# Window attention and a mixture of experts on one core: 128-row score and output matmuls on zero-blocked operands, loads placed after the stores

## The chip, the core and the metric

The kernel runs on one core of a Trainium2 chip. The metric is device time in microseconds (us). The program is executed several times, and the kernel before took 1153.46 us (median of three runs, 1153.4 to 1158.42). One further execution was recorded by the profiler. It took 1155.89 us, of which the recorded span is 1154.2.

A core has a matrix engine (TensorE, PE, with its weight loads as PEld), a vector engine (VectorE, DVE), an activation engine (ScalarE, ACT), a general engine (GpSimd, POOL), and SyncE (SP), which in this kernel only issues transfers. Transfers run on 16 DMA engines, and those that SP issues share one queue (q1). On-chip memory, SBUF, has 128 partitions, and matmul results go to PSUM.

## The reference

Attention over 8 batches of 8 heads of 576 positions of 64 values. The first four heads look at the last 32 positions, the others at every fourth of the last 128. The result, 4608 tokens of 512 values, goes to a mixture of 8 experts, of which each token uses the best two:

```python
scores = scale * np.matmul(q, k.transpose(0, 1, 3, 2))
mask_plain = (rel >= 0) & (rel < window)                                       # window 32
mask_dil = (rel >= 0) & (rel < window * dilation) & (rel % dilation == 0)      # dilation 4
attn = np.exp(scores - np.max(scores))           # of the masked scores
attn = attn / (np.sum(attn) + 1e-09)
x = np.matmul(attn, v)                           # -> 4608 x 512
noisy_logits = x @ w_gate + np.log1p(np.exp(x @ w_noise)) * noise
top2 = ...                                       # two best of 8, weights by softmax over the two
for e in range(E):
    h = np.maximum(x[mask] @ w1[e], 0.0)         # 512 -> 1024
    out[mask] += top2_w[mask, k, None] * (h @ w2[e])
```

## The kernel before

**Attention.** The work is cut into 4 units of two batches. A unit has two groups, first its dilated heads and then its plain heads, and a group has three steps. So there are 24 steps, and a step makes 384 tokens' worth of one half of x. Each step multiplies blocks of 32 queries with the 64 keys that they can see. The host has laid out the inputs so that two streams of 64 values (two heads, or two strands of the dilated positions) lie on partitions 0 to 63 and 64 to 127. All steps work with the same tiles: keys `kt`, queries `qt`, values `vd` (dilated) and `vp` (plain, two tiles, one a batch). Values carry a 65th column of ones, which gives the softmax its denominator.

**A step.** `qk` (L291, L303) puts the mask into PSUM by two matmuls with an identity of 128 rows and then adds 48 score matmuls of 64 rows, 32 queries by 64 keys. DVE takes the row maximum off (L310, L311), `expo` is ACT's exponential (L316), and `ptr` transposes on PE (L324), copied by ACT (L327). `pv` makes 48 output matmuls of 64 rows and 65 columns (L344). DVE divides by the denominator (L350, L352, L354) and so writes `x`, which has three buffers. `store_x` sends a step's x to the scratch `xs` in six transfers on SP: for each half one of 128 KB (L365) and two of 32 KB (L367). `x_transpose` (L376) and `gate_mm` (L398) make the gate's logits. The profile counts two records for a matmul of this type, so that a step shows 96 for its 48 score matmuls.

**The order.** The program is written out by hand, in a loop of 26 rounds: round i issues `qk(i)`, `expo(i-1)`, `ptr(i-1)`, the fillers of slot 2i, `store_x(i-2)`, `x_transpose(i-2)`, `pv(i-1)`, `gate_mm(i-2)` and the fillers of slot 2i+1. A filler is a piece of other work that `at(slot, ...)` put there: loads for the next groups, clearing of the output (L860, `out_rows<-zero`), filling the compaction table `tab` with defaults (L236, from the tile `free`), the staging of the first expert's weights (L579 and L565 from DRAM to `ws`; L573, L575 split them into a high and a low part). Between these, `micro()` issues single instructions of the gate: top-2 search, positions (`posp`, L499 and L502; `cnt`, L505) and the scatter of token numbers into `tab`. An index list comes back from `tab` by a transfer to `ixf`; DVE halves its entries into `ixh` (L627), and POOL gathers the rows of x for the first expert by it (L643).

**Loads.** A group's loads stand on SP's queue among the stores. `qk_loads` (L98) fetches keys and queries two groups ahead, in slot s0+5, where s0 = 6g is a group's first slot. `v_loads` (L106, L109) fetches the next group's values, in slots s0+1 and s0+2. Each is one transfer over all 128 partitions, of columns or of a whole tile.

**The experts.** From 266 us on, PE works through the experts: `up` (L697) and `down` (L738) matmuls on blocks of tokens, with high and low parts. Weights of the next expert and gathers are placed by a planner with due times (`plan`, `tick`). The first expert's first block of tokens lies in a pool `xp0` of its own, whose memory `free` uses before.

Of the kernel before, what the change touches and what calls it, by code (L numbers as in the profile page):

```python
# [24 lines left out]
FF = 1024  # L25
# [20 lines left out]
def attention_moe_kernel(ctx, tc, qt, kp, kd, vpl, vdl, w_gate, w_noise, noise, w1, w2, out, CAP=1216, SPLITS=(0, 384, 896)):  # L46
# [18 lines left out]
    xp0 = ctx.enter_context(tc.tile_pool(name="xp0", bufs=1))  # L65
# [3 lines left out]
    actx = ExitStack()  # L69
# [16 lines left out]
    VP = [vp.tile([128, 9, 4, 65], F32, name=f"vp{i}") for i in range(2)]  # L86
# [3 lines left out]
    KV = [KT[i].rearrange("p (b x s) -> p b x s", b=2, x=2 + 2 * i) for i in range(2)]  # L90
    QV = [QT[i].rearrange("p (b x s) -> p b x s", b=2, x=2 + 2 * i) for i in range(2)]

    def qk_loads(g, parts=1):
        u, ty = g // 2, 1 - g % 2
        for i in range(parts):
            for dst, src in ((KT[ty], (kp, kd)[ty][u]), (QT[ty], qt[u, ty])):
                n = dst.shape[1] // parts
                yield lambda d=dst[:, n * i:n * i + n], s=src[:, n * i:n * i + n]: sync.dma_start(d, s)  # L98

    def v_loads(g):  # L100
        u, ty = g // 2, 1 - g % 2
        if ty:
            d = VD.rearrange("p j h y c -> p (j h y c)")
            n = d.shape[1] // 3
            for i in range(3):
                yield lambda i=i: sync.dma_start(d[:, n * i:n * i + n], vdl[u, :, n * i:n * i + n])  # L106
        else:
            for b in range(2):
                yield lambda b=b: sync.dma_start(VP[b].rearrange("p j h c -> p (j h c)"), vpl[u, b])  # L109

    for f in qk_loads(0, 2):
        f()

# [100 lines left out]
    def setup_c():  # L214
# [3 lines left out]
        free = xp0.tile([128, 3072], I32, name="free", tag="raw")  # L218
        pr = free[:, 0:3 * NR].rearrange("p (a b) -> p a b", a=3)
# [10 lines left out]
        def pads(a, b):  # L230
            padt = free[:, 3 * NR:3 * NR + TC * (b - a)].rearrange("p (a b) -> p a b", b=TC)
# [6 lines left out]
        pads(0, NR // 2)  # L238
        at(12, lambda: pads(NR // 2, NR))
# [33 lines left out]
    def blocks(st, ty):  # L273

        for r in range(6):
            for w in range(2):
                a, jp = divmod(r, 3)
                if ty == 0:
                    b, ub = divmod(12 * st + 2 * r + w, 18)
                else:  # L280
                    b, ub = divmod(6 * st + 2 * jp + w, 9)
                yield r, w, a, jp, b, ub
# [3 lines left out]
    def qk(k):  # L286
        g, st = divmod(k, 3)
        ty = 1 - g % 2
        s = aps.tile([128, 2, 512], F32, name="s", tag="s")
        for y in range(2):  # L290
            tensor.matmul(s[:, y, 0:384], lhsT=identb,  # L291
                          rhs=masks[ty][:, 6 * st:6 * st + 6].rearrange("p a b -> p (a b)"),
                          start=True, stop=False, skip_group_check=True)
        for e in range(6):
            for qd in range(4):
# [6 lines left out]
                for y in range(2):  # L302
                    tensor.matmul(s[32 * qd:32 * qd + 32, y, 64 * e:64 * e + 64],  # L303
                                  lhsT=QV[ty][64 * y:64 * y + 64, b, x, 32 * ub:32 * ub + 32],
                                  rhs=KV[ty][64 * y:64 * y + 64, b, x, 32 * ub:32 * ub + 64],
                                  start=False, stop=True, skip_group_check=True)
        a = sm.tile([128, 2, 6, 64], F32, name="a")
        mx = sm.tile([128, 2, 6], F32, name="mx")
        sv = s[:, :, 0:384].rearrange("p y (e c) -> p y e c", e=6)
        vector.tensor_reduce(mx, sv, axis=AX.X, op=OP.max)  # L310
        vector.tensor_tensor(a, sv, mx.unsqueeze(3).to_broadcast([128, 2, 6, 64]), op=OP.subtract)  # L311
        SB[k] = a

    def expo(k):
        p = sm.tile([128, 2, 6, 64], F32, name="pe")
# [754 lines left out]
```

## Time and profile before

| what | value |
|---|---|
| median of three runs | 1153.46 us (1153.4 to 1158.42) |
| profiled execution: time, span | 1155.89 us, 1154.2 us |
| mean granted PE clock | 0.95 |
| PE busy | 1023.6 us (89%) |
| DVE, ACT, POOL busy | 468.6, 289.4, 509.3 us |
| first score step (mask matmul L291) | 7.87 us |
| last score step | 241.57 us |
| first `up` matmul of the experts | 265.75 us |
| SP's queue q1 | 55,520 packets, 93.22 MB |

The profile's page gives busy times of engines, and for groups of instructions the line, the engine, the operation, the tiles (written `out<-in`), their count, their busy time, the mean length of one in ns, and the idle time of the engine before them with what ended it ("releaser"). "issue" is time in which an engine waited for nothing that the profile shows. Rows of a timeline give start and length in us. SPq is SP's transfer issuing. A DMA share of 1.0 means that all 16 DMA engines were busy.

### The profile page before, as it was taken

The numbers are of one execution on the slowest core, as the hardware profiler recorded it, in microseconds if no ns is written. First come the engines' busy times: TensorE is split into PE (matmuls) and PEld (weight loads), VectorE is DVE, ScalarE is ACT, GpSimd is POOL, SyncE is SP. The second block draws the span as 40 slices with busy tenths as digits, with TensorE's granted clock in tenths as the row PEclk, the third lists the DMA queues.
The fourth block names the chain that finished last, engine by engine and source line by source line (L and its number), as shares of the span: only waits on it lengthen the run. The fifth ranks groups of instructions, "written<-read, shape, count | busy, mean of one in ns | idle before, by whom it ended". The sixth has DMA issues, their size and how long they took to land. (4 is left out here: it accounts for less than half of the span.)

```text
span 1154.2 us, 22635 instructions
## 1 busy us (share of the span) xinstructions
PE 1023.6 (89%) x9630; PEld 870.0 (75%) x9631; DVE 468.6 (41%) x1043; ACT 289.4 (25%) x540; POOL 509.3 (44%) x620
## 2 busy tenths in 40 slices
PE   6765766455889999999999999999999999999996
PEld 4554545345669878897988899888978888998895
DVE  5544353444424454334433543444343335423221
ACT  1433332252212231213122322222231223212110
POOL 3000623242836676357534654463566256542112
PEclk8898877778999999999999999999999999999998
DMA  9665555655633443434342434333343524343123
GB/s 341 233 220 189 179 190 206 198 184 177 204 71 60 117 103 92 78 80 112 75 109 49 116 62 112 85 89 73 85 109 72 111 51 112 63 112 73 19 28 43
DMA packets 78538, 135.07 MB, mean 117 GB/s; under 512 B 29168, under 2 KB 41504, under 8 KB 75616
## 3 DMA queue, kind: packets, MB, share of 16 engines
q1 hardware_dynamic: 55520, 93.22, 24.5%
q0 software_dynamic: 22912, 40.35, 19.4%
q8 instruction: 77, 1.26, 0.4%
q14 instruction: 29, 0.24, 0.1%
HBM read 92.72 MB, written 40.81 MB: 116 GB/s over the span
## 5 line engine op out<-in xcount | busy, mean ns | idle before, releaser
L697 PE MATMUL up<-x,w1h 128*128 128x512 f32 (+2 forms) x1536 | 408.7, 350 | 0.0
L650 POOL DMA_INDIRECT g<-xs,ixi x266 | 266.3, 1001 | 94.7 <-issue 76.2
L697 PEld LDWEIGHTS up<-x,w1h 128*128 128x128 f32 x1536 | 276.8, 189 | 24.5 <-DVE hl L702 0.2
L697 PE MATMUL up<-x,w1l 128*128 128x384 f32 (+2 forms) x768 | 267.6, 348 | 0.0
L715 POOL DMA_INDIRECT out_rows<-y,ixs x70 | 112.1, 1602 | 311.3 <-DVE y L747 279.4
L738 PE MATMUL dn<-w2h,hh 128*128 128x512 f32 x576 | 225.3, 391 | 1.2 <-DVE y L747 1.2
L738 PE MATMUL dn<-w2h,hl 128*128 128x512 f32 x576 | 225.2, 391 | 0.0
L738 PE MATMUL dn<-w2l,hh 128*128 128x512 f32 x576 | 225.0, 391 | 0.0
L702 DVE SCALAR_TENSOR_TENSOR hl<-up,hh 128x384 fp32r<-128x384 f32 (+2 forms) x192 | 106.8, 557 | 238.8 <-ACT hh L701 238.8
L701 ACT ACTIVATE hh<-up 128x384 fp32r<-128x384 f32 (+2 forms) x192 | 96.7, 507 | 238.7 <-PE up L697 236.2
L697 PEld LDWEIGHTS up<-x,w1l 128*128 128x128 f32 x768 | 145.1, 189 | 12.5
L539 POOL DMA_INDIRECT tab<-en,si x72 | 71.0, 987 | 126.0 <-DVE lg L437 70.5
L738 PEld LDWEIGHTS dn<-w2h,hh 128*128 128x128 f32 x576 | 108.5, 188 | 23.6 <-DVE y L747 1.6
L738 PEld LDWEIGHTS dn<-w2h,hl 128*128 128x128 f32 x576 | 108.4, 188 | 22.7
L738 PEld LDWEIGHTS dn<-w2l,hh 128*128 128x128 f32 x576 | 108.4, 188 | 22.0
L747 DVE TENSOR_SCALAR y<-dn,ixs 128x512 f32<-128x512 f32 x63 | 47.1, 750 | 143.6 <-PE dn L738 143.6
L669 ACT CAST x<-xr 128x512 fp32r<-128x512 f32 x70 | 42.0, 599 | 200.1 <-DVE xr L667 200.1
L575 DVE TENSOR_TENSOR w1l<-ws,w1h 128x1024 fp32r<-128x1024 f32 x32 | 38.9, 1215 | 82.0 <-ACT w1h L573 82.0
L573 ACT CAST w1h<-ws 128x1024 fp32r<-128x1024 f32 x32 | 33.0, 1049 | 101.5 <-DMA ws<-in_moe_w 101.5
L303 PE MATMUL s<-kt,qt 64*32 64x64 f32 x2304 | 35.1, 238 | 22.1 <-issue 21.9
L303 PEld LDWEIGHTS s<-kt,qt 64*32 64x32 f32 x2304 | 28.3, 112 | 33.3 <-issue 32.6
L670 DVE TENSOR_TENSOR x<-xr,x 128x512 fp32r<-128x512 f32 x70 | 46.2, 661 | 17.5 <-ACT x L669 17.4
(152 smaller groups left out, 809.1 us busy)
## 6 DMA issues: line engine op xcount, KB each, us to landing
ws<-in_moe_w SPq DMA_DIRECT2D x64, 512.0 KB
out_rows<-zero SPq DMA_DIRECT2D x38, 256.0 KB
vd<-in_vdl SPq DMA_DIRECT2D x12, 780.0 KB
vp<-in_vpl SPq DMA_DIRECT2D x8, 1170.0 KB
qt<-in_qt SPq DMA_DIRECT2D x7, 1152.0 KB
xs<-x SPq DMA_DIRECT2D x48, 128.0 KB
kt<-in_kp SPq DMA_DIRECT2D x4, 1216.0 KB
g<-xs,ixi POOLq DMA_INDIRECT x266
```

The costliest lines, as they stand in the source:

```text
L303: tensor.matmul(s[32 * qd:32 * qd + 32, y, 64 * e:64 * e + 64], lhsT=QV[ty][64 * y:64 * y + 64, b, x, 32 * ub:32 * ub + 32], rhs=KV[ty][64 ...
L539: ins = gpsimd.indirect_dma_start(out=tab, out_offset=bass.IndirectOffsetOnAxis(ap=si[:, kq, t:t + 1], axis=0), in_=en[:, kq, t], in_offse ...
L575: return lambda: vector.tensor_tensor(b, s, a.bitcast(F32), op=OP.subtract)
L650: gpsimd.indirect_dma_start(out=g[:, j], out_offset=None, in_=xq, in_offset=bass.IndirectOffsetOnAxis(ap=IX[e][1][:, r0 // 32 + j:r0 // 32 ...
L669: scalar.copy(xh[:, :, o:o + rn], xr[:, :, 0:rn])
L670: return lambda: vector.tensor_tensor(xl[:, :, o:o + rn], xr[:, :, 0:rn], xh[:, :, o:o + rn].bitcast(F32), op=OP.subtract)
L697: tensor.matmul(p[:, 0:n], lhsT=a[:, 128 * f:128 * f + 128], rhs=b[:, kc, 0:n], start=(i == 0), stop=(i == 11))
L701: scalar.activation(hh[:, f, 0:n], p[:, 0:n], AF.Relu)
L702: vector.scalar_tensor_tensor(hl[:, f, 0:m], p[:, 0:m], 0.0, hh[:, f, 0:m].bitcast(F32), op0=OP.max, op1=OP.subtract)
L715: ins = gpsimd.indirect_dma_start(out=out, out_offset=bass.IndirectOffsetOnAxis(ap=sc[0:rn, t, 1:2], axis=0), in_=y[0:rn], in_offset=None, ...
L738: tensor.matmul(p[0:rn], lhsT=a[:, f, o:o + rn], rhs=b[:, f % 2], start=(i == 0), stop=(i == 23))
L747: vector.tensor_scalar(y[0:rn], p[0:rn], wsc, None, op0=OP.mult)
```

## The change

Scores and outputs are computed in one matmul where there were two. The key tile gets a second axis of two: keys of the lower 64 partitions stand in block 0, those of the upper 64 in block 1, and the other half of each block is zero. A matmul over all 128 rows then gives 2 x 64 scores for 32 queries. The values get the same form, and an output matmul has 2 x 65 columns. The zeros are written once, at the start, by DVE and POOL. Loads of keys and values go to one half of the partitions at a time, queries as before. Loads of the next groups come in odd slots, after the stores of a round: values in s0+3, s0+5 and s0+7, keys and queries in two column halves in s0+7 and s0+9. The exponential is written in place, `x` has four buffers instead of three, and `pt` and `xt` one instead of two. The dilated inputs lie in a pool that is closed in slot 43; the first expert's staged weights (`wp1`) and its first block of tokens (`xp0`) are opened in its place, and the index copy and the gathers of that block come no earlier than slot 45. `free` uses the staging buffers, in three parts instead of two.

```diff
-    VD = vp.tile([128, 9, 4, 2, 65], F32, name="vd")
-    KT = [vp.tile([128, KN[i]], F32, name=f"kt{i}") for i in range(2)]
-    QT = [vp.tile([128, 4 * S], F32, name=f"qt{i}") for i in range(2)]
+    VP = [vp.tile([128, 2, 9, 4, 65], F32, name=f"vp{i}") for i in range(2)]
+    VD = dp.tile([128, 2, 9, 4, 2, 65], F32, name="vd")
+    KT = [(vp, dp)[i].tile([128, 2, KN[i]], F32, name=f"kt{i}") for i in range(2)]
...
+            n = KN[ty] // parts
+            for y in range(2):
+                yield lambda i=i, n=n, y=y: sync.dma_start(
+                    KT[ty][64 * y:64 * y + 64, y, n * i:n * i + n],
+                    (kp, kd)[ty][u, 64 * y:64 * y + 64, n * i:n * i + n])
+            n = 4 * S // parts
+            yield lambda i=i, n=n: sync.dma_start(QT[ty][:, n * i:n * i + n], qt[u, ty, :, n * i:n * i + n])
...
+                for w in range(2):
+                    yield lambda i=i, w=w: sync.dma_start(d[64 * w:64 * w + 64, w, n * i:n * i + n],
+                                                          vdl[u, 64 * w:64 * w + 64, n * i:n * i + n])
...
+    for ty in (1, 0):
+        for y in range(2):
+            (vector, gpsimd)[y].memset(KT[ty][64 * y:64 * y + 64, 1 - y], 0.0)
     for f in qk_loads(0, 2):
         f()
+
+    for v in (VD, *VP):
+        for w in range(2):
+            (gpsimd, vector)[w].memset(v[64 * w:64 * w + 64, 1 - w], 0.0)
...
-        s = aps.tile([128, 2, 512], F32, name="s", tag="s")
+        s = aps.tile([128, 8, 2, 64], F32, name="s", tag="s")
...
-                for y in range(2):
-                    tensor.matmul(s[32 * qd:32 * qd + 32, y, 64 * e:64 * e + 64],
-                                  lhsT=QV[ty][64 * y:64 * y + 64, b, x, 32 * ub:32 * ub + 32],
-                                  rhs=KV[ty][64 * y:64 * y + 64, b, x, 32 * ub:32 * ub + 64],
-                                  start=False, stop=True, skip_group_check=True)
+                tensor.matmul(s[32 * qd:32 * qd + 32, e], lhsT=QV[ty][:, b, x, 32 * ub:32 * ub + 32],
+                              rhs=KV[ty][:, :, b, x, 32 * ub:32 * ub + 64],
+                              start=False, stop=True, skip_group_check=True)
...
-        x = sm.tile([128, 2, 6, 64], F32, name="x", bufs=3)
+        x = sm.tile([128, 2, 6, 64], F32, name="x", bufs=4)
...
-                at(s0 + 1 + i // 2, f)
+                at(s0 + 3 + 2 * (i // 2), f)
         if g + 2 < 2 * U:
-            for f in qk_loads(g + 2):
-                at(s0 + 5, f)
+            for i, f in enumerate(qk_loads(g + 2, 2)):
+                at(s0 + 7 + 2 * (i // 3), f)
...
-        later(2, go)
+        d = 2 if bi else max(2, L0 + SL_W1 + 4 - slot[0])
+        later(d, go)
...
+    def open_w1():
+        dctx.close()
+        late["wp1"] = ctx.enter_context(tc.tile_pool(name="wp1", bufs=1, side="right"))
+        late["xp0"] = ctx.enter_context(tc.tile_pool(name="xp0", bufs=1, side="right"))
+    at(L0 + SL_W1 + 2, open_w1)
```

DVE's first instructions, before (`wt` is the operand of the warm-up matmuls, `ii` to `m` lead to the masks):

```order
L117 MEMSET wt 128x256
L132 TENSOR_SCALAR ii<-ii 128x1
L133 CAST ip<-ii 128x1
L138 TENSOR_SCALAR mt<-kk,ip 128x64
L139 TENSOR_SCALAR mt<-mt 128x64
```

and after:

```order
L124 MEMSET kt_98 64x2560
L124 MEMSET kt_97 64x2432
L130 MEMSET vd 64x4680
L130 MEMSET vp_94 64x2340
L130 MEMSET vp_95 64x2340
L135 MEMSET wt 128x256
L150 TENSOR_SCALAR ii<-ii 128x1
```

Five clears of half the partitions stand ahead of what the warm-up and the masks are made from. POOL has the same five, ahead of its identity matrix.

SP's transfers of the third and fourth step, before (L365 and L367 are stores, `tab<-free` the table's defaults):

```order
L98 DMA kt_95<-in_kd 128x2560
L98 DMA qt_97<-in_qt 128x2304
L236 DMA tab<-free 128x1168
L365 DMA xs<-x 4x32x256
L367 DMA xs<-x 2x32x128 x2
L365 DMA xs<-x 4x32x256
L367 DMA xs<-x 2x32x128 x2
L106 DMA vd<-in_vdl 128x1560 x3
L365 DMA xs<-x 4x32x256
L367 DMA xs<-x 2x32x128 x2
```

and after, from the second step's stores on (the stores are L381 and L383 there):

```order
L381 DMA xs<-x 4x32x256
L383 DMA xs<-x 2x32x128 x2
L381 DMA xs<-x 4x32x256
L383 DMA xs<-x 2x32x128 x2
L100 DMA kt_98<-in_kd 64x1280 x2
L104 DMA qt_100<-in_qt 128x1152
L381 DMA xs<-x 4x32x256
L383 DMA xs<-x 2x32x128 x2
L381 DMA xs<-x 4x32x256
L383 DMA xs<-x 2x32x128 x2
L100 DMA kt_98<-in_kd 64x1280 x2
L104 DMA qt_100<-in_qt 128x1152
```

Keys and queries of a group, one block of transfers before, are two blocks of three with a step's stores between them.

On DVE, the copy of the index list (`ixh<-ixf`) stood before the count of the gate's positions (`cnt<-posp`):

```order
L354 TENSOR_TENSOR x<-o,den 128x768
L627 TENSOR_SCALAR ixh<-ixf 128x6
L505 COPY cnt<-posp 128x56
L507 TENSOR_SCALAR wd<-wd 128x6
L509 RECIPROCAL wd<-wd 128x6
```

and stands after, some 35 rows later, behind the second split of the staged weights:

```order
L363 TENSOR_SCALAR den<-o 128x6 x2
L365 RECIPROCAL den<-den 128x12
L368 TENSOR_TENSOR x<-o,den 128x384 x2
L590 TENSOR_TENSOR w1l_2947<-ws,w1h_2946 128x1024
L642 TENSOR_SCALAR ixh<-ixf 128x6
L504 TENSOR_TENSOR oh<-i_165,xf 128x24
```

The copy no longer has the count of the positions behind it, and the x of two more steps is ahead of it.

More of the change, by code (lines that the diff above doesn't have):

```diff
@@ L217, in setup_c @@
         NR = ET // 16
-        free = xp0.tile([128, 3072], I32, name="free", tag="raw")
-        pr = free[:, 0:3 * NR].rearrange("p (a b) -> p a b", a=3)
+        free = [late["stage"].tile([128, FF], I32, name="free", tag="ws") for _ in range(2)]
+        pr = free[0][:, 0:3 * NR].rearrange("p (a b) -> p a b", a=3)
         pc = acon.tile([128, 2], I32, name="pc")
@@ L236, in pads @@
             sync.dma_start(tr[:, a:b], padt)
-        pads(0, NR // 2)
-        at(12, lambda: pads(NR // 2, NR))
+        for i in range(3):
+            at(6 + 6 * i, lambda i=i: pads(NR * i // 3, NR * (i + 1) // 3))
     gens, early = [], [True]
@@ L335, in pv @@
         for hh in range(4):
-            for r, w, a, jp, b, ub in blocks(st, ty):
+            for r, a, jp, b, ub in blocks(st, ty):
                 qd, c0 = (r, hh) if r < 4 else (2 * (r - 4) + hh // 2, 4 + hh % 2)
@@ L353, in pv @@
         micro(1)
-        vector.tensor_tensor(x, ov[:, :, :, 0:64], den.unsqueeze(3).to_broadcast([128, 2, 6, 64]), op=OP.mult)
+        for w in range(2):
+            vector.tensor_tensor(x[:, w].rearrange("p (b c) d -> p b c d", b=2), ov[:, w, :, :, 0:64],
+                                 den[:, w].rearrange("p (b c) -> p b c", b=2).unsqueeze(3).to_broadcast([128, 2, 3, 64]),
+                                 op=OP.mult)
         XG[k] = x
```

80 lines of the change are left out of this document (37 added, 43 removed).

## The prediction

> **What bounds the kernel now.** I read the windows by stage first, then the waits, then the transfer queue's own timeline. The windows show two kinds of time (start:end, length, busy time of PE, weight loads, DVE, ACT, POOL, then clock, DMA share, GB/s):
>
> ```profile
> 8.00:31.00 23.00, 14.15 (x541) 10.50 (x546) 12.19 (x45) 4.87 (x11) 5.41 (x12) 0.79 0.97 343
> 31.00:206.00 175.00, 113.56 (x4041) 89.76 (x4025) 77.68 (x243) 59.38 (x141) 38.68 (x73) 0.84 0.57 201
> 330.00:1154.00 824.00, 809.37 (x3959) 700.19 (x3957) 323.38 (x558) 190.34 (x318) 401.64 (x428) 0.99 0.38 82
> ```
>
> From 330 us on, PE is busy for 809 of 824 us with the experts, which the change leaves alone. Whatever it does must happen in the attention part, where PE has 61 of 175 us free and no engine is full. The waits say who is late there (engine and line, what it waited for: us in total, times, longest):
>
> ```profile
> DVE x L354 <- DMA xs<-x: 42.8, 13, 7.8
> PE pp L324 <- ACT pe L316: 22.4, 6, 9.1
> PE s L303 <- issue: 21.9, 10, 3.9
> PE xtp L376 <- DVE cnt L505: 14.2, 2, 12.4
> DVE ixh L627 <- DMA ixf<-tab: 13.3, 1, 13.3
> PE xtp L376 <- DVE x L354: 11.2, 4, 5.0
> SPq L365 <- DVE x L354: 9.6, 1, 9.6
> PE o L344 <- issue: 8.4, 7, 2.7
> ```
>
> The largest wait on work is DVE's, for the stores of x to leave a buffer. The queue that carries these stores, SP's, waited for DVE's x a single time, at the start. So the engines wait for the queue, and the queue for nobody. Its timeline shows a beat (start, length, what SP issues):
>
> ```profile
> 30.71 0.79 SPq L98 DMA_DIRECT2D kt<-in_kd  x1
> ...
> 57.75 0.64 SPq L365 DMA_DIRECT2D xs<-x  x1
> 58.44 2.03 SPq L367 DMA_DIRECT2D xs<-x  x2
> 60.51 0.69 SPq L365 DMA_DIRECT2D xs<-x  x1
> 61.24 1.99 SPq L367 DMA_DIRECT2D xs<-x  x2
> 63.33 0.82 SPq L98 DMA_DIRECT2D kt<-in_kp  x1
> ...
> 96.69 0.54 SPq L98 DMA_DIRECT2D kt<-in_kd  x1
> ...
> 159.62 0.61 SPq L98 DMA_DIRECT2D kt<-in_kd  x1
> ...
> 191.16 0.60 SPq L98 DMA_DIRECT2D kt<-in_kp  x1
> ```
>
> The keys of a group of three steps are issued at 30.71, 63.33, 96.69 and, five groups after the first, at 191.16: (191.16 - 30.71) / 5 = 32.1 us a group, 31.5 in the last ones, or 10.5 a step. The six stores of one step take 63.33 - 57.75 = 5.6 us of it, although they move little:
>
> ```profile
> 4.00:8.00 4.00, 4.00 (x20) 1.76 (x18) 2.55 (x12) 0.00 (x0) 3.28 (x8) 1.00 1.02 418
> 56.00:60.00 4.00, 3.57 (x153) 2.99 (x152) 2.67 (x8) 1.56 (x3) 0.00 (x0) 1.00 0.19 61
> 92.00:96.00 4.00, 0.00 (x0) 0.00 (x0) 0.50 (x1) 0.00 (x0) 0.00 (x0) 0.61 0.22 68
> ```
>
> Loads alone fill the transfer engines (share 1.02, 418 GB/s); in a stretch of stores the share is 0.19 to 0.22. A store therefore uses a few of the engines, and those few are what the queue waits for. In 92:96 PE did nothing at all for that reason. PE is quicker where it is left alone: its steps (mask matmuls) follow at 6.8 and 7.1 us against the queue's 10.5:
>
> ```profile
> 55.66 0.49 PE L291 MATMUL s<-mask,identb 128*128 128x384 bf16 x2
> 62.47 0.49 PE L291 MATMUL s<-mask,identb 128*128 128x384 bf16 x2
> 69.54 0.49 PE L291 MATMUL s<-mask,identb 128*128 128x384 bf16 x2
> ```
>
> The attention part ends by the same queue: the second expert matrix arrives behind it, ACT waits 12.1 us for it, and PE stands until 284:
>
> ```profile
> 280.86 1.04 ACT L586 CAST w2h<-ws 128x1024 fp32r<-128x1024 f32 x1 [12.12 <-DMA ws<-in_moe_w]
> ...
> 284.17 0.22 PE L499 MATMUL posp<-ob,tri 128*128 128x48 bf16 x1 [9.85 <-DVE ob L491]
> ```
>
> **The change, part by part.** The sum is made against the profiled execution, 1155.9 us (span 1154.2), 2.4 above the runs' median of 1153.46.
>
> *Matmuls.* Of a step's 48 score and 48 output matmuls, 24 and 24 are left, each with twice the contraction and about twice the columns. The nearest rows are the scores of now and the gate's matmuls, which have the new shape (128 rows, 32 columns of weights; 4 of 128 and 4 of 64 columns to a step):
>
> ```profile
> 53.98 0.54 PE L398 MATMUL gp<-xt,wg 128*32 128x128 f32 x16
> ...
> 56.08 1.33 PE L303 MATMUL s<-kt,qt 64*32 64x64 f32 x96
> ```
>
> Eight gate matmuls of 96 columns on average take 0.54 us, so 24 take 1.6, or by columns (128) 2.2 us, against 1.33; the outputs, 130 wide, the same against about as much. A step gets 0.6 to 1.7 us longer on PE, from 7 to 7.6 to 8.7 us. Against that half of the 30.3 us of issue waits before L303 and L344 should go with half the instructions. All of it stays under the queue's 10.5 us a step, which hides it; without that cover it is between 24 x 1.7 - 15 = 26 us lost and 24 x 0.6 - 15 = about nothing. The masks keep their columns.
>
> *Zero blocks.* DVE and POOL each clear 2560 + 2432 + 4680 + 2340 + 2340 = 14,352 elements of 64 partitions, ahead of the warm-up operand and the identity. POOL's rows give the price:
>
> ```profile
> L232 POOL MEMSET free<- 128x1168 int32 x2 | 2.1, 1066 | 30.2 <-DMA tab<-free 30.2
> L187 POOL MEMSET zero<- 128x512 f32 x1 | 0.5, 521 | 0.0
> ```
>
> (1066 - 521) / (1168 - 512) = 0.83 ns an element, so 11.9 us. Masks and scores begin 12 us later, and so does the first x:
>
> ```profile
> 17.86 0.96 DVE L354 TENSOR_TENSOR x<-o,den 128x768 f32<-128x768 f32 x1
> 18.85 0.69 SPq L365 DMA_DIRECT2D xs<-x  x1
> ```
>
> The first store goes at about 31 instead of 18.85. Now, the transfers are full until 31 (share 0.97), so most of the 12 us is covered by initial loads. But the last piece of these, one plain value tile of 1.20 MB, is put behind the first stores; at 343 GB/s it filled 3.5 us. The queue runs dry for about that: **+3.5 us**, from 0 (memsets quicker) to 12 (no cover).
>
> *Loads.* The bytes stay, by these rows:
>
> ```profile
> vd<-in_vdl SPq DMA_DIRECT2D x12, 780.0 KB
> vp<-in_vpl SPq DMA_DIRECT2D x8, 1170.0 KB
> qt<-in_qt SPq DMA_DIRECT2D x7, 1152.0 KB
> kt<-in_kp SPq DMA_DIRECT2D x4, 1216.0 KB
> kt<-in_kd SPq DMA_DIRECT2D x3, 1280.0 KB
> ```
>
> A dilated group loads 1280 + 1152 + 3 x 780 KB, a plain one 1216 + 1152 + 2 x 1170: 4.85 MB on average, 11.6 us at 418 GB/s. The beat leaves 31.5 - 3 x 5.6 = 14.7 us for loads, so 3.1 us a group go to the two changes between stores and loads, 1.6 each. The change spreads the loads over all three steps of a group, a third such place: 1.6 x 7 groups = 11 at most, nothing at least, since loads placed behind stores can also use the transfer engines that the stores leave free. I take half, **+5.5 us**. SP issues 47 more transfers at 0.4 to 0.8 us each in place of longer ones, which its queue covers (it waits for transfers, not for its own issuing); without that cover they cost 19 us at 0.4.
>
> *Half partitions.* No row shows a load into 64 partitions. At the rate of now it costs nothing. At half that rate, the keys and values before the first stores, 1280 + 2340 + 1216 + 1170 KB = 6.15 MB, take 14.7 us more at 418 GB/s; later ones, 3.67 MB a group, 8.8 us a group, 61 over seven. Here the stores help: an engine that no store uses has 5.6 us of slack a step. I take nothing, as nearest to the rows there are, and leave the rest to a rival and the range.
>
> *The fourth x buffer, the copies, the pools.* The fourth buffer shortens DVE's 42.8 us, but a buffer moves a wait and doesn't shorten the queue. The extra den and x instructions, two a step, go to a DVE that is busy for 78 of 175 us. The index copy, on which DVE stood 13.3 us and PE 12.4 (L505), moves behind two weight splits; the queue goes on through that stall. The first expert's gathers come up to four slots (two steps) later; they are due before PE's 284 us. All of this: 0, between -4 and +4.
>
> Sum: 1155.9 + 3.5 + 5.5 = 1164.9, say **1165 us**; its own range 1156 to 1178.
>
> **The rivals.** *Half-rate loads.* [...] At the start this is +14.7 in full; later the slack of the free engines takes most, and I charge a quarter of the 61, 15. 1165 + 30 = 1195, between 1175 and, if nothing is covered, 1241. For it: 418 GB/s at a share of 1.02 is a limit somewhere, and no row says on which side. Against it: the stores, not the loads, hold the queue. [...]
>
> *Faster: PE decides.* If the steps are late because PE's stalls make the stores late, half of the 30.3 us of issue waits, the 11.2 for x and the 14.2 behind the index copy go, 40.5 us, less the 12 us of the later start, with matmuls at their lower price: 1156 - 28.5 = 1127, between 1110 and, with them at the upper, 1147. It decides if the queue has gaps in which it waits for x. For it: those rows, all of them PE's. Against it: SP's single wait of 9.6 us.
>
> *No change.* The start and the bursts are both absorbed, for instance by loads that run beside stores: 1155, between 1149 and 1159.
>
> **How the numbers follow.** Forecast 0.40, half-rate loads 0.20, faster 0.24, no change 0.16. A measurement of this kernel can tell about 0.5% (5.8 us) from nothing. Faster: 0.24 and 0.02 of the no-change case, 0.26. Within 0.5%: 0.13 of that case and 0.06 of the forecast's lower edge, 0.19. Slower: 0.55. The range that leaves out the better half of the fast case and the worse half of the half-rate case is 1130 to 1198.
>
> **What would show it.** The first store of x at 29 to 33 us; SP's keys still 31 to 33 us apart per group; DVE's wait for stores shorter, but ACT's wait for the second matrix still there, ending near 290; PE's issue waits at L303 and L344 about halved with nothing gained. Half-rate loads would show as a share of 0.5 to 0.6 in the first 20 us where 1.02 stands now. I am wrong if the beat falls well under 31 us a group: then the queue wasn't the bound, or its stores and loads overlap better than they did.

## The result

The changed kernel takes 1195.59 us (median of four runs, 1194.43 to 1197.75) where the kernel before took 1155.41 beside it: a ratio of 1.0348 (95% interval 1.0315 to 1.038), 40 us slower. The forecast was 1165 us; the rival with half-rate loads had been given 1195, and the whole range was 1130 to 1198. The profiled execution of the changed kernel has a span of 1194.2 us.

In three of the five series of experiments below the kernel before itself took 1231 to 1247 us instead of 1154 to 1156, so a ratio always stands against the kernel before in the same series.

The windows of the changed kernel, by the same stages (start:end, length, busy time of PE, weight loads, DVE, ACT, POOL, clock, DMA share, GB/s):

```profile
8.00:31.00 23.00, 11.57 (x132) 6.15 (x132) 15.53 (x28) 1.64 (x2) 15.38 (x27) 1.00 1.02 245
31.00:206.00 175.00, 109.64 (x2107) 90.43 (x2107) 77.12 (x279) 53.54 (x127) 32.16 (x62) 0.84 0.69 174
```

The transfer engines are as busy from 8 to 31 us as they were (share 1.02, before 0.97) and move 245 GB/s instead of 343. In the attention part the share went up from 0.57 to 0.69 while the rate fell from 201 to 174: more engine time for the same bytes (over the whole span the queue q1 takes 28.1% of the 16 engines for 93.23 MB, before 24.5% for 93.22). SP's keys (now in two column halves a group, of which the first is shown) show the beat:

```profile
52.98 1.23 SPq L100 DMA_DIRECT2D kt<-in_kd  x2
88.68 1.16 SPq L100 DMA_DIRECT2D kt<-in_kp  x2
127.68 1.23 SPq L100 DMA_DIRECT2D kt<-in_kd  x2
161.12 1.17 SPq L100 DMA_DIRECT2D kt<-in_kp  x2
199.91 1.26 SPq L100 DMA_DIRECT2D kt<-in_kd  x2
232.97 1.18 SPq L100 DMA_DIRECT2D kt<-in_kp  x2
```

(232.97 - 52.98) / 5 = 36.0 us a group, where 31.5 to 32.1 stood. The waits of the first 330 us (engine and line, what it waited for: us in total, times, longest):

```profile
PE s L317 <- DMA qt<-in_qt: 58.6, 11, 11.2
PE pp L336 <- ACT a L328: 20.4, 4, 18.3
PE wm L141 <- DVE ii L150: 16.5, 1, 16.5
ACT w2h L601 <- DMA ws<-in_moe_w: 14.8, 1, 14.8
PE o L356 <- ACT pt L339: 7.9, 17, 1.9
```

DVE no longer waits for stores, and PE's issue waits before scores are 3.5 us where 21.9 stood (first row below, after the idle time). In their place PE waits 58.6 us for queries, the last piece of each batch of loads. The experts' first matmul starts at 304.8 us instead of 265.75, 39 us later, so nearly the whole loss is made before it:

```profile
L317 PE MATMUL s<-kt,qt 128*32 128x128 f32 x1152 | 49.4, 325 | 62.1 <-DMA qt<-in_qt 58.6 <-issue 3.5
...
L712 PE MATMUL up<-x,w1h x1536: 307/334/775, 304.8 to 1148.8; 128*128 128x384 f32 x64, 128*128 128x512 f32 x64, 128*128 128x320 f32 x64
```

(The second row is the summary of one line's instructions: shortest, median and longest in ns, then first and last start in us.)

### The profile page after: what moved, and what is told of

The parts are those of the page before. It is cut to its first block, busy times and chain, and to the rows that moved or that the text cites. A ratio compares the mean times of both kernels' runs of the same rounds, so it can differ in the third digit from the quotient of the medians.

```text
span 1194.2 us, 18188 instructions
## 1 busy us (share of the span) xinstructions
PE 1032.6 (86%) x7326; PEld 880.6 (74%) x7327; DVE 484.7 (41%) x1101; ACT 288.5 (24%) x540; POOL 522.9 (44%) x626
## 3 DMA queue, kind: packets, MB, share of 16 engines
q1 hardware_dynamic: 57952, 93.23, 28.1%
q0 software_dynamic: 22912, 40.35, 18.5%
## 4 chain that ended last, share of the span: by engine, by line
PE 75%; DMA 10%; SPq 5%; DVE 4%; issue 4%; ACT 1%; POOL 0%; POOLq 0%; DVEq 0%; ACTq 0%
PE up L712 35%; PE dn L753 31%; DMA qt<-in_qt 5%; SPq L383 3%; PE s L317 2%; DMA ws<-in_moe_w 2%; PE o L356 1%; PE dn L749 1%; PE dn L747 1%; DMA g<-xs,ixh 1%; SPq L381 1%; PE pp L336 1%; SPq L100 1%; DMA vp<-in_vpl 1%; DMA vd<-in_vdl 1%
## 5 line engine op out<-in xcount | busy, mean ns | idle before, releaser
L712 PEld LDWEIGHTS up<-x,w1l 128*128 128x128 f32 x768 | 145.2, 189 | 12.4
L317 PE MATMUL s<-kt,qt 128*32 128x128 f32 x1152 | 49.4, 325 | 62.1 <-DMA qt<-in_qt 58.6
L317 PEld LDWEIGHTS s<-kt,qt 128*32 128x32 f32 x1152 | 39.7, 130 | 72.2 <-issue 57.4
L684 ACT CAST x<-xr 128x512 fp32r<-128x512 f32 x70 | 41.9, 599 | 201.9 <-DVE xr L682 201.9
L322 DVE TENSOR_REDUCE mx<-s 128x12 f32<-128x768 f32 x24 | 23.0, 957 | 95.5 <-PE s L317 95.5
```

The lines of the kernel that those rows point to most:

```text
L317: tensor.matmul(s[32 * qd:32 * qd + 32, e], lhsT=QV[ty][:, b, x, 32 * ub:32 * ub + 32], rhs=KV[ty][:, :, b, x, 32 * ub:32 * ub + 64], star ...
L684: scalar.copy(xh[:, :, o:o + rn], xr[:, :, 0:rn])
L712: tensor.matmul(p[:, 0:n], lhsT=a[:, 128 * f:128 * f + 128], rhs=b[:, kc, 0:n], start=(i == 0), stop=(i == 11))
```

## The experiments

Theory 1: a transfer into 64 neighbouring partitions moves at about half rate, and the queue, which sets the beat, pays for it. Theory 2: the loss comes from where the loads stand, behind the stores, and from the new matmuls. The later start is a third part. The forecast's own theory, that the stores hold the queue because they use few transfer engines, was tested too.

| run | what | ratio (interval) | the kernel before there |
|---|---|---|---|
| b_low | before, keys and values loaded in lower and upper halves | 1.0374 (1.032 to 1.0428) | 1245 us |
| b_evn | before, in even and odd partitions | 1.0017 (0.9983 to 1.0052) | 1245 us |
| a_again | changed kernel, unaltered | 1.0069 (1.0023 to 1.0114) | 1231 us |
| a_evn2, a_evn3 | changed, even and odd partitions | 1.0025 (0.9986 to 1.0064), 1.0006 (0.9972 to 1.0039) | 1231, 1247 us |
| a_evn4 | the same | 1.0104 (1.0086 to 1.0122) | 1156 us |
| a_evn_place | the same, loads where the kernel before has them | 1.0038 (1.0015 to 1.0062) | 1154 us |
| a_place | changed, loads where the kernel before has them | 1.0123 (1.0071 to 1.0175) | 1247 us |
| a_evn_start | as a_evn4, zeros in another order | 1.0133 (1.0111 to 1.0154) | 1154 us |
| b_st16, b_st16_2, b_st16_3 | before, stores of 128 rows | 1.0016, 1.0017, 1.0001 (all within 0.9968 to 1.0061) | 1245, 1231, 1247 us |
| b_st16_4 | the same | 0.9663 (0.964 to 0.9687) | 1156 us |
| a_evn_st16 | as a_evn4, with such stores | 0.9805 (0.9756 to 0.9853) | 1231 us |
| a_all | the same, zeros as in a_evn_start | 0.972 (0.9699 to 0.9741) | 1154 us |
| a_best_p | with such stores, loads as before, zeros in a third order | 0.9855 (0.9812 to 0.9897) | 1247 us |
| a_best2 | with such stores, loads as in the change, POOL clears more | 0.9704 (0.9688 to 0.9721) | 1156 us |

**Halves of the partitions, in the kernel before.**

```diff
+    def two(d, s):
+        d, s = d.rearrange("(y p) n -> y p n", y=2), s.rearrange("(y p) n -> y p n", y=2)
+        for y in range(2):
+            sync.dma_start(d[y], s[y])
...
-                yield lambda i=i: sync.dma_start(d[:, n * i:n * i + n], vdl[u, :, n * i:n * i + n])
+                yield lambda i=i: two(d[:, n * i:n * i + n], vdl[u, :, n * i:n * i + n])
```

The diff is cut: keys and plain values are changed in the same way. b_evn has "(p y) n -> y p n" in `two`.

> The kernel before with one edit: each load of keys and of values is issued as two transfers, partitions 0 to 63 and 64 to 127 (queries and everything else unchanged). Theory 1 (a transfer into 64 neighbouring partitions moves at about 245 GB/s instead of 418, as the first 31 us of the changed kernel suggest): 7.35 MB of initial keys and values take 30.0 instead of 17.6 us, +12 at the start, and 3.67 MB a group 15.0 instead of 8.8 us, +6 for each of seven groups less what the stores cover: 1180 to 1210 us. Theory 2 (the loss of the changed kernel comes from where its loads stand and from its matmuls, not from the halves): 1153 to 1162 us, the price of 35 more transfers at most.

> As the run with partitions 0 to 63 and 64 to 127, with the same number of transfers of the same sizes, but the two halves are the even and the odd partitions. Theory 1, if what counts is how far over the partitions a transfer is spread: 1153 to 1162 us, as before. If what counts is that a transfer has 64 partitions, or that there are more transfers: the same time as the run with neighbouring halves, 1180 to 1210 us by theory 1's price. Theory 2: 1153 to 1162 us for both.

Measured 1292.3 us and 1247.2 us, with the kernel before at 1245.1: the neighbouring halves cost 3.7%, the even and odd ones nothing that can be measured, at the same number of transfers of the same sizes. From 12 to 28 us, in which both kernels mostly load (b_evn's first stores start at 20.63 us), the windows read (first b_low, then b_evn):

```profile
12.00:28.00 16.00, 7.57 (x227) 4.88 (x228) 4.60 (x7) 2.38 (x3) 1.55 (x4) 0.59 1.04 194
```

```profile
12.00:28.00 16.00, 9.79 (x354) 7.60 (x355) 7.03 (x22) 3.98 (x6) 1.55 (x4) 0.79 1.03 353
```

Both keep all transfer engines busy (1.04, 1.03); one moves 194 GB/s and the other 353. The keys' issues, of b_low and of b_evn:

```profile
49.30 1.84 SPq L96 DMA_DIRECT2D kt<-in_kd  x2
...
161.47 1.66 SPq L96 DMA_DIRECT2D kt<-in_kp  x2
```

```profile
31.91 1.87 SPq L96 DMA_DIRECT2D kt<-in_kd  x2
...
127.93 1.28 SPq L96 DMA_DIRECT2D kt<-in_kp  x2
```

Three groups take 112.2 us (37.4 each) with neighbouring halves, and 96.0 (32.0 each) with even and odd ones, after a start that is 17.4 us later. The experts' first matmul stands at 342.7 and 302.1 us, so 40.6 of the 54.5 us between the two profiled executions are lost before it. So theory 1 holds, and the number of partitions isn't what counts: 64 neighbouring ones got 194 GB/s, every second one of 128 got 353. (The rows that a transfer reads in DRAM change along with the partitions, here and in the runs below, so no run says on which side the limit is.)

**Even and odd partitions in the changed kernel.**

```diff
-                    KT[ty][64 * y:64 * y + 64, y, n * i:n * i + n],
-                    (kp, kd)[ty][u, 64 * y:64 * y + 64, n * i:n * i + n])
+                    KT[ty].rearrange("(d y) z n -> y d z n", y=2)[y][:, y, n * i:n * i + n],
+                    (kp, kd)[ty][u].rearrange("(d y) n -> y d n", y=2)[y][:, n * i:n * i + n])
...
-            (vector, gpsimd)[y].memset(KT[ty][64 * y:64 * y + 64, 1 - y], 0.0)
+            (vector, gpsimd)[y].memset(KT[ty][:, 1 - y], 0.0)
```

The diff is cut: values are changed in the same way, the host writes its streams interleaved, and the exponential writes its two windows interleaved into a tile of its own. Loads of keys and values wait for the zeros of their tile here, and at the start the queries come first. (a_evn, a first form in which the transposes were to undo the interleaving, gave no time.)

> The changed kernel unaltered, beside the kernel before on this chip, as the base for the other runs here: a ratio of 1.035 if this chip is like the first; on a chip where the kernel before takes 1245 us and stands 83 us in issue waits before its score and output matmuls, the change halves the instructions there and loses less: a ratio of 0.99 to 1.02.

> The changed kernel with the two streams of keys, queries and values on even and odd partitions in place of the lower and upper 64 (the host lays the inputs out so, the exponential writes its two windows interleaved, the zeros are cleared over all partitions before the loads). Loads stay behind the stores, the matmuls have the new form. Theory 1 (transfers into 64 neighbouring partitions run at about 245 GB/s): the beat falls from 36 to 31 to 33 us a group, and the time by 25 to 40 us against the changed kernel, to a ratio of 1.00 to 1.01 against the kernel before. Theory 2 (the place of the loads behind the stores): the ratio stays within 1.0 percent of the changed kernel's, with waits of the score matmuls for queries near 58 us.

> The changed kernel with even and odd partitions once more, for a chip on which the kernel before takes 1153 us. Of the changed kernel's ratio of 1.035, theory 1 (half-rate loads) puts 25 to 32 us here: a ratio of 1.005 to 1.012, a beat of 32.6 us a group, and the rest, some 5 to 12 us, is the late start and the place of the loads. If more than half of the loss is the place behind the stores, the ratio stays above 1.018.

> The changed kernel with even and odd partitions, for a chip on which the kernel before takes 1153 us, with the same numbers as in the run before this: a beat of 32.6 us a group and a ratio of 1.005 to 1.012 if the half rate is 25 to 32 of the 40 us; above 1.018 if the place of the loads is more than half. On a chip where the kernel before takes 1230 us or more: 1.00 again.

With the kernel before at its usual time: 1.0104 in place of the changed kernel's 1.0348. The halves' rate, with these smaller edits, is thus 2.4%, 28 us (by the two intervals, 24 to 33). The beat of a_evn4 is that of the kernel before again:

```profile
51.38 1.21 SPq L100 DMA_DIRECT2D kt<-in_kd  x2
...
207.87 1.18 SPq L100 DMA_DIRECT2D kt<-in_kp  x2
```

(207.87 - 51.38) / 5 = 31.3 us. Where the kernel before took 1231 us, the changed kernel lost only 0.7%, and a_evn2 0.3%. There too the experts' first matmul came earlier with even and odd partitions, at 294.8 us (a_evn2) instead of 317.0 (a_again), but of these 22 us only 8 were left at the end (medians 1233.8 and 1241.6 us); why is open. Theory 2 alone is out, but it keeps a share.

**The place of the loads.**

```diff
-                at(s0 + 3 + 2 * (i // 2), f)
+                at(s0 + 1 + i // 4, f)
...
-            for i, f in enumerate(qk_loads(g + 2, 2)):
-                at(s0 + 7 + 2 * (i // 3), f)
+            for f in qk_loads(g + 2):
+                at(s0 + 5, f)
```

> The changed kernel with even and odd partitions, and with the loads of keys, queries and values put where the kernel before has them (keys and queries in slot s0+5, all columns at once, values in s0+1 and s0+2). If the place behind the stores costs, the waits of score matmuls for queries (19 us) go and the beat falls from 32.6 to 31.7 us a group, together 5 to 15 us. If the place is worth something (loads beside stores): 5 to 15 us slower. If neither: within 5 us of the run with even and odd partitions, a ratio of 1.00.

> The changed kernel with its loads into the lower and upper 64 partitions, but put where the kernel before has them (slot s0+5, and s0+1 and s0+2). Against the changed kernel this shows what the place is worth while loads run at half rate. Theory 1: the bytes in the queue are the same, the beat stays at 35 to 37 us a group and the ratio at 1.025 to 1.035. If the place behind the stores makes the loads late by itself: the waits for queries (58.6 us) fall under 25 and the ratio to 1.005 to 1.02.

On even and odd partitions the old place gives 1.0038 where the new one gives 1.0104: 0.7%, some 8 us (4 to 11 by the intervals). Its beat is (197.16 - 40.28) / 5 = 31.4 us, no other than a_evn4's:

```profile
40.28 1.88 SPq L100 DMA_DIRECT2D kt<-in_kd  x2
...
197.16 1.25 SPq L100 DMA_DIRECT2D kt<-in_kp  x2
```

So the place does not cost by the beat of the loads. The steps of PE show where it costs. The table has the start of a step's mask matmul in us (steps are counted from 1; the last row is the experts' first matmul):

| step | before | changed | a_evn4 | a_evn_place |
|---|---|---|---|---|
| 1 | 7.9 | 23.3 | 23.1 | 24.4 |
| 7 | 55.7 | 61.8 | 59.0 | 61.9 |
| 10 | 79.6 | 87.5 | 81.2 | 81.5 |
| 12 | 104.1 | 118.8 | 107.5 | 99.7 |
| 22 | 206.4 | 234.1 | 209.6 | 203.1 |
| 23 | 227.3 | 251.3 | 224.4 | 215.8 |
| 24 | 241.6 | 283.7 | 252.7 | 245.9 |
| experts | 265.8 | 304.8 | 273.9 | 268.5 |

Up to the tenth step a_evn4 and a_evn_place run alike. There a_evn4, which issues the step's queries behind the stores of one step more, waits 9.7 us for them, and a_evn_place 1.9 (first a_evn4, then a_evn_place):

```profile
84.07 0.58 SPq L104 DMA_DIRECT2D qt<-in_qt  x1
...
91.38 2.79 PE L319 MATMUL s<-kt,qt 128*32 128x128 f32 x48 [9.68 <-DMA qt<-in_qt]
```

```profile
73.58 0.58 SPq L104 DMA_DIRECT2D qt<-in_qt  x1
...
83.88 1.52 PE L319 MATMUL s<-kt,qt 128*32 128x128 f32 x48 [1.92 <-DMA qt<-in_qt]
```

Two steps later a_evn4 is 7.8 us behind, and still 6.5 at the 22nd step. This one late load accounts for about the whole difference. Over the whole attention part PE waits 41.9 us for queries in a_evn4 and 24.9 in a_evn_place.

a_place ran where the kernel before took 1247 us, and the unaltered changed kernel was not run beside it (a_again's 1.0069 is of another series). Its result falls between the two expectations: 18.5 us of waits for queries and a ratio of 1.0123 are as the second said (a_again waits 27.2 us), the beat as the first: (197.48 - 46.77) / 4 = 37.7 us, near b_low's 37.4 with neighbouring halves, with the loads in their old place.

```profile
46.77 1.43 SPq L100 DMA_DIRECT2D kt<-in_kd  x2
...
197.48 1.26 SPq L100 DMA_DIRECT2D kt<-in_kd  x2
```

**The start.** a_evn_start clears the dilated keys first, then makes warm-up operand, identity and masks, and then clears the rest, the dilated values ahead of the plain tiles (the diff is cut):

```diff
+    zero_k(1)
...
     gpsimd.tensor_copy(identb, ident)
+    gpsimd.memset(VD[:, 1], 0.0)
...
         masks.append(m)
+        if ty == 1:
+            vector.memset(VD[:, 0], 0.0)
+    zero_k(0)
```

> The changed kernel with even and odd partitions, and with the zero blocks cleared in the order in which they are needed: first the dilated keys', then the warm-up operand, identity and masks, and the values' and plain keys' beside or behind them. Theory 1 (start): the first x is stored at 20 to 25 us instead of 33.9, and the attention part ends 6 to 12 us earlier than with the zeros first, a ratio of about 0.99 against the kernel before where the zeros first give 1.0025. Theory 2 (the initial loads hide the zeros anyway): no more than 4 us.

It was a miss: 1.0133, no better than a_evn4's 1.0104, and the first store of x at 38.91 us in place of 33.74. The masks came earlier, but the loads of dilated values, which wait for their zeros here, came later, and DVE's first maximum (26.61) stands behind its clears:

```profile
11.81 4.45 DVE L176 CAST mask<-m 128x64 bf16<-128x64 f32 x6
15.30 3.96 DVE L184 MEMSET vd<- 128x4680 f32 x1
19.71 2.08 DVE L126 MEMSET kt<- 128x2432 f32 x1 [0.46 <-issue]
22.23 2.01 DVE L188 MEMSET vp<- 128x2340 f32 x1 [0.44 <-issue]
24.68 2.01 DVE L188 MEMSET vp<- 128x2340 f32 x1 [0.44 <-issue]
26.61 0.89 DVE L330 TENSOR_REDUCE mx<-s 128x12 f32<-128x768 f32 x1
```

**The stores.** The scratch xs gets its rows in another order, so that the 128 KB store writes 128 rows that follow each other; the token numbers in the table are computed to match.

```diff
-            dst = xs[r0:r0 + 384, 256 * ty:256 * ty + 256].rearrange("(r w q) c -> w r q c", w=2, q=32)[w]
-            sync.dma_start(dst[0:4], x[:, w, 0:4].rearrange("p h d -> p (h d)"))
+            dst = xs[r0 + 192 * w:r0 + 192 * w + 192, 256 * ty:256 * ty + 256]
+            sync.dma_start(dst[0:128], x[:, w, 0:4].rearrange("p h d -> p (h d)"))
```

> The kernel before with rows of the scratch xs in another order, so that the 128 KB store of a half step writes 128 rows that follow each other (the token numbers in the table are changed to match; the two 32 KB stores stay as they are). If the stores hold the queue because they use few transfer engines, a 128 KB store shrinks from about 1.4 to about 0.4 us of the queue's time, 2 us a step, the beat from 31.5 to 25 to 28 us a group, and the time to 1110 to 1130 us, until PE at 7 us a step is the bound. If the queue's time is not the stores' (or PE decides): 1150 to 1160 us.

> The kernel before with rows of the scratch xs in another order, so that a 128 KB store writes 128 rows that follow each other, once more. On a chip where the kernel before takes 1153 us, where its steps follow the queue: 2 us a step less in the queue, the beat from 31.5 to 25 to 28 us, a ratio of 0.96 to 0.98. On a chip where it takes 1245 us and its issue waits set the steps: 1.00 again.

> The kernel before with the 128 KB stores on 128 rows that follow each other, for a chip on which the kernel before takes 1153 us. Before, the first stretch up to 112 us showed a beat of 28 us where 31.6 stood. If stores hold the queue and PE has room: 27 to 28 us a group, 20 to 30 us in all, a ratio of 0.975 to 0.983. If PE's issue waits (half as many instructions in the changed kernel) take over: 0.99 to 1.0, and then it is the changed kernel's matmuls that make the stores' gain come through.

> The kernel before with the 128 KB stores on 128 rows that follow each other. On a chip where the kernel before takes 1153 us: 0.975 to 0.983 if the stores hold its queue and PE has room for the gain, 0.99 to 1.0 if PE's issue waits take over. Where it takes 1230 us or more: 1.00 again, with a stretch of some 25 us in which PE gets a matmul every 0.7 us or more.

With the kernel before at 1156 us it gives 0.9663: 39 us less, 1117.3 us, as the first of these expectations said (1110 to 1130) and more than the last two, and the fastest kernel of this study. The bytes, the number of transfers and the queue are the same. The beat falls to 24.6 to 29.1 us:

```profile
28.52 1.56 SPq L98 DMA_DIRECT2D kt<-in_kd  x1
56.01 0.80 SPq L98 DMA_DIRECT2D kt<-in_kp  x1
81.76 0.51 SPq L98 DMA_DIRECT2D kt<-in_kd  x1
106.34 0.63 SPq L98 DMA_DIRECT2D kt<-in_kp  x1
133.54 0.34 SPq L98 DMA_DIRECT2D kt<-in_kd  x1
162.65 0.40 SPq L98 DMA_DIRECT2D kt<-in_kp  x1
```

Now the queue waits for DVE's x (30.7 us in eight waits), and DVE has no wait for the stores left. From 31 to 206 us the engines' share is 0.69 at 242 GB/s, where the kernel before had 0.57 at 201:

```profile
SPq L376 <- DVE x L365: 30.7, 8, 10.2
```

```profile
31.00:206.00 175.00, 121.00 (x4370) 94.98 (x4348) 91.40 (x297) 65.24 (x155) 47.08 (x86) 0.88 0.69 242
```

That the form of the stores held the queue is thus shown; that it did so by using few of the engines is argued from the share, for no run counts the engines of one store. Where the kernel before took 1231 to 1247 us, the same edit gained nothing three times: PE stood 67.7 to 81.2 us in issue waits before its score matmuls there, against 16.6 in b_st16_4. Why is open.

**All together.** Stores, even and odd partitions, and three orders of the zeros. a_evn_st16 is a_evn4 with these stores; a_all is a_evn_start with them; a_best_p clears dilated keys and values, makes the masks and clears the rest, with the loads where the kernel before has them; in a_best2 POOL alone clears that rest, and the loads are behind the stores (a_best2's order, cut):

```diff
+    zero(KT[1])
...
+    zero(VD)
...
         masks.append(m)
+    for v in (KT[0], *VP):
+        gpsimd.memset(v, 0.0)
```

> Both edits in the changed kernel: even and odd partitions, and stores of 128 rows that follow each other. With half-rate loads and slow stores gone from the queue, PE sets the steps at 7.6 to 8.7 us, and the issue waits are halved: a ratio of 0.94 to 0.98 against the kernel before, and the fastest of these. If the loads behind the stores are late whatever they cost: 1.00 to 1.02.

> Even and odd partitions, stores of 128 rows that follow each other, and the zeros in the order of their need. Without the start's 12 us the run with both edits (ratio 0.9805, first experts' matmul at 278 us) should give 0.970 to 0.975 and 266 to 270 us. If the stores' queue is not behind it and only the start's loads count: 0.98 again.

> Even and odd partitions, stores of 128 rows, loads put where the kernel before has them, and the zeros of dilated keys and values first, then the masks, then the plain ones. Against the run with the loads behind the stores (ratio 0.972, where the zeros were in another order and the first store went at 37.5 us): first store at 24 to 28 us, a beat of 23 to 25 us, a ratio of 0.958 to 0.968. If the place before the stores is worse once PE sets the steps: 0.97 or more.

> Even and odd partitions, stores of 128 rows, loads behind the stores, and the zeros of dilated keys and values first, then the masks; POOL alone clears the plain keys and values, so that DVE goes from the masks to the first softmax (in the last such run it stood 6 us in these clears). First store at 24 to 29 us in place of 33.8 to 37.5, a beat of 24 to 25 us, a ratio of 0.960 to 0.970 on a chip like the first, 0.975 on one like the others; if the plain loads, which wait for POOL, hold the first stores back: 0.972 and more.

a_evn_st16 gave 0.9805, where b_st16_2 in the same series gave 1.0017, and a_best_p 0.9855, where b_st16_3 gave 1.0001. a_all gave 0.972 and a_best2 0.9704, with the kernel before at its usual time. a_all's ratio is the one expected, but not in the way expected: the experts begin at 236.8 us and not at 266 to 270, and the start is no earlier. The first store stands at 37.45 us in a_all, and at 33.84 and 34.92 in a_best_p and a_best2, where 24 to 29 were expected; both ratios missed their range, a_best2's closely. In a_best2 DVE's six small copies of masks take 8.42 us, with POOL's clears placed right behind its part of the masks, against 0.70 in the kernel before (first row; the second is the kernel before's):

```profile
13.14 8.42 DVE L175 CAST mask<-m 128x64 bf16<-128x64 f32 x6
```

```profile
6.02 0.70 DVE L156 CAST mask<-m 128x64 bf16<-128x64 f32 x6
```

In one series, b_st16_4 takes 1117.3 us and a_best2 1121.8. With the stores out of the way the kernel with the old matmuls is no slower as a whole than the one with the new, though the new have no issue waits to speak of:

```profile
L331 PE MATMUL s<-kt,qt 128*32 128x128 f32 x1152 | 42.8, 302 | 12.4 <-DMA qt<-in_qt 12.0 <-issue 0.4
```

```profile
L314 PE MATMUL s<-kt,qt 64*32 64x64 f32 x2304 | 36.7, 242 | 16.8 <-issue 16.6
```

(a_best2, then b_st16_4.) But a_best2 begins its first step at 16.1 us and b_st16_4 at 8.1; at the 23rd step it is 11.5 us ahead (190.0 against 201.5), and at the 24th 5.6 behind (215.9 against 210.3). In between its ACT waits 17.6 us before it copies the first expert's weights, with the 23rd step's exponential behind that copy; b_st16_4's has no such wait. So these runs don't show that the new matmuls are worth nothing, nor that the gain in the steps is theirs: loads, buffers and zeros differ as well.

**b_again** is the kernel before, run once for its profile, beside a_all and the runs of that series. It gave 1156.59 us, with the experts' first matmul at 266.6.

> The kernel before, unaltered, for its profile on a chip of this series of runs. If what made the change look cheaper on the second chip is that chip's slower instruction issue, the beat of the keys' loads is 31 to 33 us in the first five groups as on the first chip, the issue waits of PE before score and output matmuls come to 60 us or more against 30, and the experts begin at 295 to 305 us against 266. On a chip like the first: 266 us and a time of 1150 to 1160.

## Why the prediction was wrong

The direction was right and the size was not: 40 us where 9 to 12 had been summed. The stated range holds 1195.59 near its upper end, the sum does not. By its own steps:

**What bounds the kernel** was right. Loads made slower with the work of PE, DVE, ACT and POOL left as it was cost 3.7% (b_low), and stores made faster gain 3.4% (b_st16_4).

**Half partitions** is the step that failed: "I take nothing, as nearest to the rows there are". It measured 28 us (24 to 33). The half rate that the step priced (+14.7 us at the start, 61 later) and the rival's charge rests on was a supposition, which no row of the kernel before showed; the runs showed 245 GB/s in the changed kernel against 343 before in the same window, and 194 (b_low) against 353 (b_evn). The rival's +30 is near what was found, but by luck, as its two parts were wrong in opposite directions: between the changed kernel and a_evn4 the steps are 2.8 us apart at the seventh and 24.5 at the 22nd, and the keys' beat is 36.0 against 31.3 us, 4.7 of the 8.8 us a group that the step priced. So little of the 14.7 came, since the zeros hold the start of both, and about half of the 61, where the rival charged a quarter. The mistake was to let the absence of a row count as a row for no cost. Every load of keys, queries and values in the profile spanned 128 partitions, so the profile couldn't speak for either end. With no row against it, half rate deserved more than 0.20; a single half alone was not run. What was to show it was also wrong: the share was to fall to 0.5 or 0.6, and from 8 to 31 us it stayed at 1.02 while the rate fell to 245. The sign that did show it was the beat, 36.0 us where 31 to 33 had been said.

**Loads** was priced at +5.5 us by a third change between stores and loads in each group. The price is near (8 us, 4 to 11), the mechanism wasn't: the beat with even and odd partitions is 31.3 and 31.4 us, whichever place the loads have. One batch of queries comes late to PE instead.

**Zero blocks** was priced at +3.5 us, what is left of 12 when the initial loads cover the rest; no run has the zeros alone. Masks and scores begin 15.5 us later (7.87 and 23.34 us), not 12, and the first store stands at 33.93 us where about 31 was said. By the seventh step 6.1 us of it are left (a_evn_place 6.2), so the cover is there. a_evn_place, in which neighbouring halves and new place are gone, is 4.4 us slower than the kernel before (1.0038); the zeros and all else that the change does are in this number.

**Matmuls** were hidden, as forecast. The issue waits before scores went from 21.9 to 3.5 us, more than by half, and the time did not follow. In a_evn_place the steps even gain: from 6.2 us behind the kernel before at the seventh step to 11.5 ahead at the 23rd, in part because the stall on the index copy (12.4 us of PE) is gone. At the 24th it is 4.3 behind. The 23rd step's exponential stands on ACT behind the copy of the first expert's weights, and SP issues the second of their loads at 233.58 us here and at 227.98 in the kernel before (first row the kernel before, second a_evn_place):

```profile
234.55 1.04 ACT L573 CAST w1h<-ws 128x1024 fp32r<-128x1024 f32 x1 [6.08 <-DMA ws<-in_moe_w]
```

```profile
239.02 1.04 ACT L591 CAST w1h<-ws 128x1024 fp32r<-128x1024 f32 x1 [22.13 <-DMA ws<-in_moe_w]
```

So the attention part ends by the queue, as the prediction read it, and the rival in which PE decides is out for this kernel. What the new matmuls are worth by themselves stays open.

**The fourth x buffer, the copies, the pools** were put at 0, between -4 and +4. DVE's 42.8 us of waits for stores are gone and PE waits for queries, as "a buffer moves a wait" had it; no run changed the buffer alone. The stall on the index copy is gone too, but the one behind ACT's first weight copy, 7.5 us of PE in the kernel before, is 18.3 in the changed one:

```profile
276.07 1.04 ACT L588 CAST w1h<-ws 128x1024 fp32r<-128x1024 f32 x1 [23.65 <-issue]
277.02 0.84 ACT L328 ACTIVATE a<-a 128x768 f32<-128x768 f32 x1
```

The terms 28 + 8 + 4.4 make 40 us, the loss of the changed kernel, and must do so, since each is the step from one kernel to the next (changed, a_evn4, a_evn_place, before). The first two are differences between series, and their intervals are wide.

## What to carry to other kernels

Where a transfer queue sets the beat, look at the form of each transfer and at the partitions that it reaches, not only at its bytes: here six small stores a step held the queue, and a new order of rows in a scratch gained 3.4% where a rewrite of the matmuls, with the loads and zeros that it needed, lost 3.5%. Loads into half of the partitions, if they set the pace, should take every second partition and not a run of 64 neighbours (353 GB/s in b_evn against 194 in b_low, whose rows in DRAM were spread and neighbouring likewise). And where no row of a profile shows a form that a change brings in, the missing row is no evidence for the cheap end.

## What the runs showed of the hardware that was not expected

With loads of the same sizes and number, 194 GB/s were moved where they went into the lower or upper 64 partitions (b_low) and 353 GB/s where they went into the even or odd ones (b_evn, both from 12 to 28 us), at a DMA share of 1.04 and 1.03. Here the share thus said for how long engines were occupied, and not how much they moved; share and rate had to be read together.

Six small copies on DVE took 8.42 us (a_best2) and 4.45 us (a_evn_start, a_best_p) with POOL's clears placed beside them (in a_best_p the copies start at 13.14 us, and POOL clears from 13.27 to 19.58), and 0.70 in the kernel before and in the changed kernel. The POOL of the changed kernel has cleared its keys and values by 13.15 us, and the copies start at 20.75. That the clears are the cause was not tried.
